# Second product of a gated recurrence and SiLU block: seven half-size products against three one-pass products of exact parts

## The chip, the cores and the metric

The kernel runs on one core of a Trainium2 chip. The time is device microseconds of that core for one execution of the whole program. Names used below: TensorE (PE; PEld is its weight load), VectorE (DVE), ScalarE (ACT), GpSimd (POOL) and SyncE (SP), which only issues transfers.

## The reference

Two blocks follow one another. The first is a complex gated recurrence over 768 steps, for 4 batches of 8 heads with 48 dimensions; the second is a two-layer network with SiLU on the 3072 tokens:

```python
scale = np.minimum(mag, 0.999) / (mag + 1e-06)        # mag = |a_re + i a_im|
for t in range(S):
    new_re = ar * S_re - ai * S_im
    new_im = ar * S_im + ai * S_re
    S_re, S_im = (new_re + kv, new_im)                # kv: outer product of k[t], v[t]
    y[:, :, t] = np.einsum('bhd,bhde->bhe', q[:, :, t], S_re)
x = attn_out.transpose(0, 2, 1, 3).reshape(B * S, H * D)   # 3072 x 384
h = x @ w_in                                          # 384 x 2048: the first product
g = h * (1.0 / (1.0 + np.exp(-h)))
return (g @ w_out).astype(np.float32)                 # 2048 x 384: the second product
```

## The kernel before, in words

The sequence is cut into 24 chunks of 128 tokens (n = 0 to 23), the chunks into 12 pairs of 256 tokens (p = 0 to 11). A chunk's recurrence is worked out in a parallel form: magnitudes and angles of the gates on ACT and VectorE (`G0` to `Ga`), running sums of both by TensorE (`L`, `phase`), sines (`trig`), exponentials (`exp`), rotated and scaled q and k (`K`, `Q`), their transposition to T (`tk` and `tq` on VectorE in 32x32 blocks, then 12 transfers `td` from the SP and POOL queues), scores (`w`), a mask on VectorE (`m`), and the output `y` from scores and the state S carried over from four chunks before. ACT copies `y` to xT (`x`), and six small transfers (`xd`) put its last third in place.

For each pair the network then runs in 8 steps (jp = 0 to 7), each over 256 of the 2048 hidden values. `h:p.jp` (L706) is six float32 matmuls of TensorE, which leave twelve records; `g` (L715) is SiLU on ACT into a tile of 128x512; `r:p.jp` (L745) adds the step's part of the second product into PSUM. There are two kinds of `r`. For the first two pairs it is straight: four float32 matmuls of 384 columns (L756). From the third pair on (`WINO = 2`, L110) it is the method of halves (L777): the 256 tokens by two blocks of 128 hidden values, and those by two halves of 192 columns, are treated as a 2x2 by 2x2 product that takes seven products of half size in place of eight (L803, 14 records). It needs four sums of blocks of `g` on VectorE for each step (`gs`, L736), combinations of the weights made once (`wc`, `wl`), and seven additions for each pair when the last step is done (`of`, L807). Every float32 matmul appears as two records.

Chunks from the eighth on have their running sums made from two exact parts: L425 rounds a tile to float32r, L426 takes the rest, and L437 multiplies both parts with a triangle of ones or halves, which a float32r matmul does in one record.

The order of the work is written out by hand as a list of tokens (L912 on); every engine runs its own instructions in the order of that list, and so does every queue of transfers. Weights arrive as pairs of 32-bit words and are turned into float32 at the start (`F` fetches, `R`, `H` and `J` convert). `sm` and `lk` look at the weights once more near the end; a branch after the list falls back to another routine when inputs are extreme.

PSUM has two buffers for `h` (`p_h`), two for attention (`p_m`) and four for the results (`p_o`, later `late_o`). Most tiles of attention have two buffers each. A helper, L292, records every ACT function, and L286 every load of an ACT table.

Of the kernel before, what the change touches and what calls it, by code (L numbers as in the profile page):

```python
# [70 lines left out]
def kernel(  # L71
# [38 lines left out]
    WINO = 2  # L110
    STRAIGHT = 4
    FULL = 6

# [38 lines left out]
    def load_a(n, g, name):  # L152
        p, i = divmod(n, 2)
        if name not in A[p]:
            A[p][name] = flat(pre.tile([C, 2, H, D], F32, tag=name, name=f"{name}{p}", bufs=2))
        b, c = place(n)
        queue_of(g).dma_start(
            out=cut(A[p][name], i).rearrange("p (h d) -> p h d", d=D),
            in_=(a_re if name == "re" else a_im)[b].rearrange("h (c p) d -> p c h d", p=C)[:, c])
# [18 lines left out]
    w2 = consts.tile([C, NJ, DM], F32)  # L178
# [5 lines left out]
    for s in range(DF // WC):  # L184
# [3 lines left out]
        for j in range(s * WC // C, (s + 1) * WC // C):  # L188
            blocks.append((w2[:, j], (2, j // 2), [(0, w_out[ts(j, C)])]))
# [48 lines left out]
    def small(n):  # L238
# [3 lines left out]
        if n < NT and w.dtype != F32:  # L242
            raw = pre.tile([C, 2, H, D], F32, tag=("re", "im")[n % 2], name=f"small{n}", bufs=2)
# [175 lines left out]
    def in_two(n, x):  # L419
# [3 lines left out]
        t = room("left").tile([C, 2, DM], F32R, tag="part", name=f"{x}_parts{n}", bufs=2)  # L423
# [15 lines left out]
    def carry(n):  # L439
        if place(n)[1] > 0:  # L440
            X[n]["carry"] = att.tile([1, DM], F32, tag="carry", name=f"carry{n}")
# [9 lines left out]
    def turn(n):  # L451
        x = X[n]
        ps = x["phase"]
        x["turn"] = att.tile([C, DM], F32, tag="turn", name=f"turn{n}")
# [91 lines left out]
    def squared(n, i):  # L546
        x = X[n]
        if "sq" not in x:
            x["sq"] = room("left").tile([C, NB, 2 * H, Q], F32, tag="sq", name=f"sq{n}", bufs=2)
# [165 lines left out]
    def silu(p, jp):  # L715
        g = moe.tile([C, 2, T], F32, tag="g", name=f"g{p}_{jp}", bufs=4)
        special(g, A[p]["h", jp], AF.Silu)
        A[p]["g", jp] = g
# [3 lines left out]
    w2v = w2.rearrange("p (j i) (n c) -> p i n j c", i=2, n=2)  # L722

    def combined():

        wc = later["wc"] = room("right").tile([C, 3, NJ // 2, DM // 2], F32, tag="wc", name="wc")
        for out, a, b, op in ((wc[:, 2], w2v[:, 1, 1], w2v[:, 0, 1], ALU.subtract),
                              (wc[:, 1], wc[:, 2], w2v[:, 0, 0], ALU.add),
                              (wc[:, 0], w2v[:, 1, 0], wc[:, 1], ALU.subtract)):
            nc.vector.tensor_tensor(out=out, in0=a, in1=b, op=op)  # L730

    def combined_last():
        nc.vector.tensor_tensor(out=w2v[:, 0, 1], in0=w2v[:, 0, 1], in1=w2v[:, 0, 0],
                                op=ALU.subtract)

    def sums_of(p, jp):  # L736
        g = A[p]["g", jp]
        a11, a12, a21, a22 = (g[:, i, ts(m, C)] for m in range(2) for i in range(2))
        t = room("right").tile([C, 4, C], F32, tag="gs", name=f"gs{p}_{jp}", bufs=2)
        for i, a, b, op in ((0, a21, a22, ALU.add), (1, a11, a21, ALU.subtract),  # L740
                            (2, t[:, 0], a11, ALU.subtract), (3, a12, t[:, 2], ALU.subtract)):
            nc.vector.tensor_tensor(out=t[:, i], in0=a, in1=b, op=op)  # L742
        A[p]["gs", jp] = t

    def result(p, jp):  # L745
        if p >= WINO:
            result_of_halves(p, jp)
            return
        if jp == 0:
            A[p]["o"] = [p_o.tile([C, 2, DM // 2], F32, tag="o",  # L750
                                                                  name=f"o{p}_{m}")
                         for m in range(2)]
        for m in range(2):
            for ji in range(2):
                j = jp * 2 + ji
                nc.tensor.matmul(A[p]["o"][m].rearrange("p n c -> p (n c)"),  # L756
                                 lhsT=A[p]["g", jp][:, ji, ts(m, C)], rhs=w2[:, j],
                                 start=(j == 0), stop=(j == NJ - 1))

    def finish(p):  # L760
        if p >= WINO:
            combine(p)
            return
        for m in range(2):
            ot = moe.tile([C, 2, DM // 2], F32, tag="ot", name=f"ot{p}_{m}")
            nc.scalar.copy(out=ot, in_=A[p]["o"][m])
            store(p, m, {m: ot})

    def store(p, m, ot, half=None):

        b, c = place(2 * p + m)
        to, of = out[ts(b * NCH + c, C)], ot[m].rearrange("p n c -> p (n c)")
        if half is not None:
            to, of = to[:, ts(half, DM // 2)], ot[m][:, half]
        (nc.sync if half is not None else nc.scalar).dma_start(out=to, in_=of)

    def result_of_halves(p, jp):  # L777
        if jp == 0:
            A[p]["o"] = [late_o().tile([C, 2, DM // 2], F32, tag="o", name=f"o{p}_{m}")
                         for m in range(4)]  # L780


        pairs = (0, 5, 4, 3, 1, 6, 2)
        o = [A[p]["o"][i // 2][:, i % 2] for i in map(pairs.index, range(7))]
        final = jp == NJ // 2 - 1
        if p == NP - 1 and jp == NJ // 2 - 2:
            return


        merged = final and p == NP - 1  # L790
        todo = [(i, j) for i in (pairs if merged else range(7))
                for j in ((jp - 1, jp) if merged else (jp,))]
        if merged:

            todo.insert(2, todo.pop(todo.index((1, jp - 1))))
        for i, j in todo:
            g, t = A[p]["g", j], A[p]["gs", j]
            products = ((g[:, 0, 0:C], w2v[:, 0, 0, j]), (g[:, 1, 0:C], w2v[:, 1, 0, j]),
                        (g[:, 1, C:T], later["wc"][:, 0, j]), (t[:, 0], w2v[:, 0, 1, j]),
                        (t[:, 1], later["wc"][:, 2, j]), (t[:, 2], later["wc"][:, 1, j]),  # L800
# [391 lines left out]
```

## Time and profile before

Three runs took 644.46, 644.66 and 646.29 us, median 644.66.

| of the profiled execution | |
|---|---|
| its own time | 644.93 us |
| its span, first to last instruction | 643.2 us |
| mean granted TensorE clock | 0.997 |
| TensorE busy | 628.2 us, 4084 records |
| VectorE busy | 471.1 us, 1009 instructions |
| ACT busy | 360.4 us, 530 instructions, 97.5 of it 76 table loads at L286 |
| GpSimd busy | 212.7 us |
| first product, L711 | 1152 records, 259.5 us |
| second product, straight (L756) and of halves (L803) | 128 and 1120 records |
| sums of `g`, L742 | 320 instructions of 128x128 |
| additions at a pair's end, L816 | 70 instructions of 128x192 |
| transfers | 73.31 MB, 166,224 of 183,447 packets under 512 B |

Busy times of different rows on one engine can overlap, since a matmul is recorded from its start to the end of its way through the array. The mean duration of a record is therefore longer than the time by which it holds up the next one; that time is read from the start of one record to the start of the next. "Idle before" in a row of groups is the time in which the engine stood still ahead of it, with the work that released it.

### The profile page before, as it was taken

The page shows a single profiled execution, that of the slowest core. Times are in us where ns is not written, and L with a number is a line of the kernel's source. Part 1 is how long each engine was busy: PE and PEld are TensorE (multiplying, and loading weights), DVE is VectorE, ACT ScalarE, POOL GpSimd, SP SyncE. Part 2 cuts the span into 40 slices and gives each one's busy share as a digit, 9 for nine tenths or more (in the row PEclk, how much of TensorE's full clock was granted, in tenths as well). Part 3 has the DMA queues.
Part 4 walks back from the last instruction along what each step waited for, and adds up shares of the span by engine and source line. Part 5 has one row for each costly group of instructions (what it writes and reads, how often), then busy time and mean ns, then how long its engine had stood idle before and what let it go on. Part 6 is the DMA issues. An engine that isn't in the chain of part 4 may idle for free.

```text
span 643.2 us, 11607 instructions
## 1 busy us (share of the span) xinstructions
PE 628.2 (98%) x4084; PEld 561.3 (87%) x4084; DVE 471.1 (73%) x1009; ACT 360.4 (56%) x530; POOL 212.7 (33%) x368
## 2 busy tenths in 40 slices
PE   6898999999999999999999999999999999999997
PEld 4777777778999999999999899899999899999996
DVE  5997578885786975896897786776797686585554
ACT  7994777864566666756587258419447542421200
POOL 7442102433553325142063153360352224242000
PEclk9899999999999999999999999999999999999999
DMA  9677474743674476481474554665375438558680
GB/s 168 133 180 160 132 196 133 130 75 73 137 102 81 95 113 99 89 111 26 91 104 68 102 79 64 121 92 89 61 134 79 106 46 162 108 119 175 213 285 29
DMA packets 183447, 73.31 MB, mean 114 GB/s; under 512 B 166224, under 2 KB 171816, under 8 KB 183384
## 3 DMA queue, kind: packets, MB, share of 16 engines
q1 hardware_dynamic: 168424, 50.79, 38.1%
q0 software_dynamic: 11648, 17.20, 17.3%
q10 hardware_dynamic: 3312, 4.52, 1.9%
q8 instruction: 34, 0.56, 0.4%
q14 instruction: 29, 0.24, 0.1%
HBM read 48.90 MB, written 4.79 MB: 83 GB/s over the span
## 4 chain that ended last, share of the span: by engine, by line
PE 84%; ACT 6%; DVE 4%; DMA 3%; issue 1%; SPq 0%; ACTq 0%; POOL 0%; DVEq 0%; POOLq 0%
PE h L711 35%; PE o L803 27%; PE o L756 7%; PE a L569 6%; PE y L596 3%; PE y L599 3%; ACT s L292 1%; ACT L286 1%; DMA v<-in_v_dram 1%; ACT mag L292 1%; PE s L667 1%; DMA xT<-y 1%; PE phase L437 1%; DVE ot L816 1%; PE L L437 1%
## 5 line engine op out<-in xcount | busy, mean ns | idle before, releaser
L711 PE MATMUL h<-xT,w 128*128 128x256 f32 x1152 | 259.5, 379 | 1.0 <-DMA xT<-y 0.6
L711 PEld LDWEIGHTS h<-xT,w 128*128 128x128 f32 x1152 | 217.0, 190 | 31.8 <-ACT g L292 1.2
L292 ACT ACTIVATE g<-h 128x512 f32<-128x512 f32 x96 | 56.2, 595 | 157.8 <-PE h L711 138.7
L557 POOL DMA_DIRECT2D T<-sq x120 | 77.5, 653 | 102.8 <-PE o L803 32.5
L286 ACT ACT_TABLE_LOAD x76 | 97.5, 1283 | 13.5 <-DVE ot L816 8.6
L503 POOL DMA_DIRECT2D dec<-ends x48 | 30.7, 644 | 149.5 <-DMA ends<-eq 141.6
L803 PE MATMUL o<-w,gs 128*128 128x192 f32 x320 | 77.9, 326 | 0.0
L803 PE MATMUL o<-w,g 128*128 128x192 f32 x320 | 66.2, 329 | 0.0
L803 PE MATMUL o<-wc,gs 128*128 128x192 f32 x320 | 64.9, 326 | 0.0
L685 POOL DMA_DIRECT2D S<-ssq x84 | 46.0, 555 | 37.7 <-DVE ssq L674 28.4
L803 PEld LDWEIGHTS o<-w,gs 128*128 128x128 f32 x320 | 56.3, 190 | 0.1
L742 DVE TENSOR_TENSOR gs<-g 128x128 f32<-128x128 f32 x160 | 38.7, 282 | 23.8 <-ACT g L292 18.5
L803 PEld LDWEIGHTS o<-w,g 128*128 128x128 f32 x320 | 53.6, 190 | 2.7 <-issue 0.7
L803 PEld LDWEIGHTS o<-wc,gs 128*128 128x128 f32 x320 | 54.2, 190 | 0.0
L569 PE MATMUL a<-T 96*128 96x128 f32 x384 | 50.3, 278 | 0.8 <-ACT T L561 0.3
L577 DVE TENSOR_TENSOR w<-a,upto_r 128x512 f32<-128x512 f32 x48 | 32.7, 687 | 24.8 <-PE a L569 22.1
L569 PEld LDWEIGHTS a<-T 96*128 96x128 f32 x384 | 47.3, 191 | 3.8 <-issue 1.1
L756 PE MATMUL o<-w,g 128*128 128x384 f32 x128 | 43.6, 488 | 0.0
L608 POOL DMA_DIRECT2D xT<-y x30 | 14.9, 504 | 84.5 <-ACT y L644 84.5
L803 PE MATMUL o<-wc,g 128*128 128x192 f32 x160 | 38.9, 326 | 0.0
L756 PEld LDWEIGHTS o<-w,g 128*128 128x128 f32 x128 | 24.0, 190 | 15.2 <-issue 0.4
L816 DVE TENSOR_TENSOR ot<-o,ot 128x192 f32<-128x192 f32 x70 | 21.5, 351 | 20.5 <-ACT ot L812 14.5
(121 smaller groups left out, 971.2 us busy)
## 6 DMA issues: line engine op xcount, KB each, us to landing
T<-sq SPq DMA_DIRECT2D x120, 64.0 KB
T<-sq POOLq DMA_DIRECT2D x120, 64.0 KB, 4.2
raw<-in_moe_w_out_dram SPq DMA_DIRECT2D x16, 384.0 KB
small<-in_moe_w_in_dram SPq DMA_DIRECT2D x16, 384.0 KB
small<-in_moe_w_out_dram SPq DMA_DIRECT2D x16, 384.0 KB
raw<-in_moe_w_in_dram SPq DMA_DIRECT2D x24, 192.0 KB
out_dram<-ot ACTq DMA_DIRECT2D x23, 192.0 KB
im<-in_a_im_dram SPq DMA_DIRECT2D x16, 192.0 KB
```

The source lines that it names most:

```text
L286: nc.scalar.preload_act_table_set(SETS[of][0])
L292: nc.scalar.activation(out=out, in_=in_, func=func, **kw)
L503: nc.gpsimd.dma_start(out=x["dec"][a * D:(a + 1) * D], in_=ends[n].rearrange("(h d) -> d h", d=D))
L557: (nc.gpsimd if a % 2 else nc.sync).dma_start(out=to[ts(b, Q), :, a], in_=X[n]["sq"][ts(a, Q), b])
L569: nc.tensor.matmul(ps[:, h], lhsT=x["kT"][:, hh * HH + h], rhs=x["qT"][:, hh * HH + h], start=True, stop=True)
L577: nc.vector.tensor_tensor(out=x["w", hh], in0=x["a", hh], in1=upto.unsqueeze(1).to_broadcast([C, HH, C]), op=ALU.mult)
L685: (nc.gpsimd if g % 2 else nc.sync).dma_start(out=to[ts(b, Q), r, :, e], in_=sq[ts(g, Q), :, b, 0:e.stop - e.start])
L711: nc.tensor.matmul(ps[:, ji], lhsT=w1[:, dc, ts(jp * 2 + ji, C)], rhs=A[p]["xT"][:, dc], start=(dc == 0), stop=(dc == ND - 1))
L742: nc.vector.tensor_tensor(out=t[:, i], in0=a, in1=b, op=op)
L756: nc.tensor.matmul(A[p]["o"][m].rearrange("p n c -> p (n c)"), lhsT=A[p]["g", jp][:, ji, ts(m, C)], rhs=w2[:, j], start=(j == 0), stop=(j ...
L803: nc.tensor.matmul(o[i], lhsT=a, rhs=b, start=(jp == 0 and i < 4), stop=(final and j == jp and i in ((5, 3, 6, 2) if p == NP - 1 else (4, ...
L816: nc.vector.tensor_tensor(out=to, in0=a, in1=b, op=ALU.add)
```

## The change

From the fourth pair on (`PARTS = 3`) the second product is taken apart differently; the third pair becomes straight, and the halves with their sums, combinations and additions are gone. Each of `g` and the weights is split into a head (its bits above the lowest twelve) and a rest. With the rest of the weights scaled by 4096 ("fine"), the heads rounded to float32r ("coarse", "head"), and two differences `d` (of `g`) and `t` (of the weights), two accumulators are formed for each chunk: v from d·t, and u from head·coarse plus tail·fine. The result is (1 + 1/4096)·u − v/4096. Every operand is float32r, so that each step has twelve one-pass matmuls of 384 columns.

For each step VectorE makes the head (`ga`), the tail (`gb`) and the difference (`gc`), and ACT copies the head to float32r (`gr`). The three forms have one buffer each (`PBUF = 1`); in the last pair some steps use buffers of attention that are free by then (`HOMES`). The weights' parts are made once (`wh`, `wq`, `wd`, `ws`, `we`); their differences are kept in DRAM (`wk`), and each step loads its difference from there, 384 KB on the SP queue into one of two buffers (`lw`). The end of a pair is a multiplication on ACT (`ov`) and one fused operation on VectorE (`oj`) for each chunk, in two halves for the last pair. `re`, `im`, `part`, `sq`, `turn` and `carry` get one buffer in place of two, and `w2` becomes a ring of nine tiles. The whole list of tokens is in a new order.

```diff
-    WINO = 2
+    PARTS = 3
+    FINER = 2.0 ** -12
...
+    GBUF = 4
+    PBUF = 1
...
-    w2 = consts.tile([C, NJ, DM], F32)
+    w2_pool = Ring(consts, NJ // 2 + 1)
+    w2 = [w2_pool.tile([C, 2, DM], F32, tag="w2", name=f"w2_{jp}") for jp in range(NJ // 2)]
...
-            x["sq"] = room("left").tile([C, NB, 2 * H, Q], F32, tag="sq", name=f"sq{n}", bufs=2)
+            x["sq"] = room("left").tile([C, NB, 2 * H, Q], F32, tag="sq", name=f"sq{n}", bufs=1)
...
+    def head(dst, src):
+        nc.vector.tensor_scalar(out=dst.bitcast(I32), in0=src.bitcast(I32), scalar1=-4096,
+                                scalar2=None, op0=ALU.bitwise_and)
+
+    def difference(dst, tail, whole):
+        nc.vector.scalar_tensor_tensor(out=dst, in0=tail, scalar=-1 / FINER, in1=whole,
+                                       op0=ALU.mult, op1=ALU.add)
+
+    HOMES = (0, 1, 2, 0, 2, 0, 1, 1)
...
+    def w_head(jp):
+        W["head", jp] = temp(f"w_head{jp}", 2 * DM)
+        head(W["head", jp], w2[jp])
+
+    def w_rounded(jp):
+        nc.scalar.copy(out=coarse(jp), in_=W["head", jp])
...
+        nc.vector.tensor_tensor(out=W["rest", jp], in0=w2[jp], in1=W["head", jp], op=ALU.subtract)
...
+        difference(t, W["rest", jp], W["head", jp])
...
+        nc.scalar.mul(t, W["rest", jp], 1 / FINER)
...
+        nc.sync.dma_start(out=second_d[jp].bitcast(I32), in_=W["diff", jp].bitcast(I32))
+
+    def w_loaded(p, jp):
+        t = A[p]["diff", jp] = room("right").tile([C, 2, DM], F32R, tag="diff",
+                                                  name=f"diff{p}_{jp}", bufs=2)
+        nc.sync.dma_start(out=t.bitcast(I32), in_=second_d[jp].bitcast(I32))
+
+    def g_form(p, jp, name):
+        home_of = HOMES[jp] if p == NP - 1 else 0
+        if home_of == 0:
+            t = room("right").tile([C, 2, T], F32R, tag=name, name=f"{name}{p}_{jp}", bufs=PBUF)
...
+    def g_head(p, jp):
+        A[p]["temp", jp] = temp(f"g_head{p}_{jp}", 2 * T)
+        head(A[p]["temp", jp], A[p]["g", jp])
+
+    def g_rounded(p, jp):
+        nc.scalar.copy(out=g_form(p, jp, "head"), in_=A[p]["temp", jp])
+
+    def g_tail(p, jp):
+        t = g_form(p, jp, "tail")
+        nc.vector.tensor_tensor(out=t, in0=A[p]["g", jp], in1=A[p]["temp", jp], op=ALU.subtract)
+
+    def g_diff(p, jp):
+        difference(g_form(p, jp, "gd"), A[p]["tail", jp].bitcast(F32), A[p]["temp", jp])
...
+    def result_of_parts(p, jp):
+        x = A[p]
+        a, b, d, t = (x[name, jp] for name in ("head", "tail", "gd", "diff"))
+        last_ = jp == NJ // 2 - 1
+        for m in range(2):
+            u, v_ = (x["o"][2 * m + i].rearrange("p n c -> p (n c)") for i in range(2))
+            for ji in range(2):
+                nc.tensor.matmul(v_, lhsT=d[:, ji, ts(m, C)], rhs=t[:, ji],
+                                 start=(jp == 0 and ji == 0), stop=(last_ and ji == 1))
+            for ji in range(2):
+                j = jp * 2 + ji
+                nc.tensor.matmul(u, lhsT=a[:, ji, ts(m, C)], rhs=W["coarse"][:, j],
+                                 start=(jp == 0 and ji == 0), stop=False)
+                nc.tensor.matmul(u, lhsT=b[:, ji, ts(m, C)], rhs=W["fine", jp][:, ji],
+                                 start=False, stop=(last_ and ji == 1))
...
+    def o_scaled(p, m):
+        ot = A[p]["ot", m] = moe.tile([C, 2, DM // 2], F32, tag="ot", name=f"ot{p}_{m}")
+        nc.scalar.mul(ot, A[p]["o"][2 * m + 1], -FINER)
+
+    def o_joined(p, m):
...
+            nc.vector.scalar_tensor_tensor(out=ot[:, n], in0=u[:, n], scalar=1 + FINER,
+                                           in1=ot[:, n], op0=ALU.mult, op1=ALU.add)
...
+                gr:7.3 turn:19 lw:7.3 w:17.1 m:17.1 v:17 y:17 x:17 gb:7.3 gc:7.3 g:7.7 G7:10 G4:10
+                s:17 ss:17 r:7.3 td:18 w:18.1 w:18.0 lw:7.4 gb:7.4 gr:7.4 gc:7.4 r:7.4 k:19 xd:8
...
+                lw:11.4 lk:30 lk:31 ck2:0 ck3:0 ck4:0 h:11.4 gr:11.6 r:11.6 g:11.4 h:11.7 ga:11.5
+                ga:11.4 gr:11.4 gb:11.4 gc:11.4 r:11.4 g:11.7 ga:11.7 gb:11.5 gc:11.5 lw:11.5
+                gb:11.7 gc:11.7 gr:11.5 r:11.5 gr:11.7 lw:11.7 r:11.7 ov:11.0 ov:11.1 oj:11.0
+                oj:11.1
```

## The prediction

> **What bounds the kernel now.** I read the page first: the busy shares and the chain that ended last.
>
> ```profile
> PE 628.2 (98%) x4084; PEld 561.3 (87%) x4084; DVE 471.1 (73%) x1009; ACT 360.4 (56%) x530; POOL 212.7 (33%) x368
> PE   6898999999999999999999999999999999999997
> PE 84%; ACT 6%; DVE 4%; DMA 3%; issue 1%; SPq 0%; ACTq 0%; POOL 0%; DVEq 0%; POOLq 0%
> PE h L711 35%; PE o L803 27%; PE o L756 7%; PE a L569 6%; PE y L596 3%; PE y L599 3%; ACT s L292 1%; ACT L286 1%; DMA v<-in_v_dram 1%; ACT mag L292 1%; PE s L667 1%; DMA xT<-y 1%; PE phase L437 1%; DVE ot L816 1%; PE L L437 1%
> ```
>
> TensorE holds 84% of the chain, the second product (L803, L756) 34%. Busy time can't tell TensorE's rate, so I take the rate from where it runs without a gap, in the chain in order of time:
>
> ```profile
> 101.03 2.58 PE o L756 x8
> ...
> 164.62 4.55 PE o L803 x28
> 169.17 2.59 PE h L711 x12
> ```
>
> One `r` of halves is 14 records: 4.55/2 = 2.275 us, 162.5 ns each. A straight `r` is 2.58 us (322.5 ns a record); an `h` 2.59 us (216 ns). From 60.76 us on, at the first `r`, the chain is nearly all TensorE. The busy times by stage say how near the others are:
>
> ```profile
> core 0: us, PE busy (x) PEld busy (x) DVE busy (x) ACT busy (x) POOL busy (x), PEclk, DMA share, GB/s
> 300.00:350.00 50.00, 50.00 (x331) 47.16 (x331) 42.84 (x96) 33.81 (x48) 18.40 (x33) 1.00 0.55 88
> 400.00:450.00 50.00, 49.51 (x347) 46.25 (x345) 34.50 (x77) 25.16 (x39) 15.22 (x27) 1.00 0.60 97
> ```
>
> TensorE is full, VectorE has 7 to 15 us of 50 free. Shortening a product shortens the end, as long as VectorE keeps ahead.
>
> **What the Trainium skill says.** "TensorE: Matmul & The Clock Gate", "Back-to-back issue gap", gives a warm matmul N/2.4 + 2.5 ns: 162.5 ns for 384 columns. Two-pass records agree (322.5 is twice 161). "VectorE: DVE Perf Modes", the perf-mode tier table, has float32 `tensor_scalar` at twice the rate of `tensor_tensor`; the trace agrees (432 against 692 ns at 512 elements, below). "DMA: Bandwidth & Descriptors", "Issuing engines are not separate DMA queues": all queues share 16 engines, so the new loads meet the rearranging of T and S.
>
> **The change, part by part.** *TensorE.* The one-pass form exists before: the exact parts of L437, two records of 384 columns. Two timeline answers around 206 us:
>
> ```profile
> 205.45 0.38 PE L711 MATMUL h<-xT,w 128*128 128x256 f32 x1
> 205.48 0.70 PE L437 MATMUL phase<-th_parts,upto_r 128*128 128x384 f32 x2
> ```
> ```profile
> 205.85 0.33 PE L437 MATMUL phase<-th_parts,upto_r 128*128 128x384 f32 x1
> 206.02 0.59 PE L711 MATMUL h<-xT,w 128*128 128x256 f32 x2
> ```
>
> From 205.45 to 206.02 is 0.57; less the 0.216 of the `h` it is 0.354 for two, 177 ns each (the second alone 170). No row shows more than two in sequence. If the surplus over 162.5 belongs to the change of form, twelve in sequence take 1.95 us; if to each matmul, 2.12. I take 170 ns, 2.04 us. Gain: 72 × (2.275 − 2.04) = 16.9 us. The third pair goes back to the straight product: 8 × (2.58 − 2.275) = 2.4 us lost. Net −14.5 (ends −21.0 and −8.7). `h`, `w`, `y`, `s`, L and phase keep their numbers, and ACT's table loads stay the same within one (counted along both orders).
>
> *VectorE and ACT.* Rows used, by line and shape:
>
> ```profile
> L742 DVE TENSOR_TENSOR gs<-g 128x128 f32<-128x128 f32 x160 | 38.7, 282 | 23.8 <-ACT g L292 18.5 <-PE o L803 5.1
> L577 DVE TENSOR_TENSOR w<-a,upto_r 128x512 f32<-128x512 f32 x48 | 32.7, 687 | 24.8 <-PE a L569 22.1 <-PE y L596 2.5
> L816 DVE TENSOR_TENSOR ot<-o,ot 128x192 f32<-128x192 f32 x70 | 21.5, 351 | 20.5 <-ACT ot L812 14.5 <-DMA xT<-y 3.9 <-PE o L803 0.6
> L49 DVE SCALAR_TENSOR_TENSOR w<-raw,w 128x512 int32<-128x512 int32 x12 | 8.3, 692 | 0.4
> L401 DVE TENSOR_SCALAR re<-re 128x768 f32<-128x768 f32 x11 | 6.2, 566 | 0.0
> L47 DVE TENSOR_SCALAR w<-raw 128x512 int32<-128x512 int32 x12 | 5.2, 432 | 1.9 <-DMA raw<-in_moe_w_in_dram 1.9
> L561 ACT COPY T<-tp 96x512 f32<-96x512 f32 x16 | 8.5, 583 | 0.9 <-PE tp L541 0.9
> ```
>
> Per product VectorE gets `ga` 0.43, `gb` 0.69 and `gc` 0.69, 1.81 us, for four sums of 0.28 to 0.29, 1.14: +0.67, ×72 = 48.2. Per pair two `oj` of 0.56 replace seven additions of 0.351: −1.34, ×9 = −12.1. The third pair loses its sums and additions: −11.6. The weights cost 8 × (0.566 + 0.955 + 0.955) = 19.8 (L401; 128x768 like L333), less `wc` and `wl`, 7.0. Sum +37: VectorE 471 to 508. ACT gets 72 × 0.58 + 16 × 0.84 + 20 × 0.48 − 10 × 0.32 = +62: 360 to 422. Both are hidden behind TensorE so long as they keep up. Summing start-to-start costs (0.36, 0.70, 0.61 for the three parts; other tokens likewise) along the new order from r:3.0 to r:9.0, VectorE has 278 us of work and TensorE 299: 93%, where before it was 76%.
>
> *The new wait.* With PBUF = 1 `gb`, `gc` and `gr` of a product start after the product before has been read. Queued behind a waiting `gb` on VectorE are the masks (`w`), T's transposes and `ut`/`ul` of later chunks, for which `y` and phase wait. After the release `gb` and `gc` take 1.3 us plus a semaphore; the order puts at least an `h` (2.6), `w:18` pair (1.8) or `y` (1.85) there, except between products of the last pair, which have other homes. Over the 63 intervals up to r:10.7 I took VectorE's work from one `gb` to the next against TensorE's from one product to the next: at the row costs none waits, eleven are left with under 0.7 us spare, the least 0.34. With VectorE's costs 7% up the waits sum to 2.6 us, with 10% to 8 us. Since this count leaves out VectorE's own waits, I put 3 us (ends 0 and 10).
>
> *Loads.* 72 loads of 384 KB (28 MB) and 8 stores. The nearest, `small`, are issued at 617.99 and reduced at 621.23, 3.2 us; in dense sequence they come about 1 us apart. 72 × 1 us raises the DMA share from about 0.55 to 0.67. Two buffers give a load the time from product k−2's end to product k: 9.4 us on average, at least 6.5 up to the eleventh pair, so it is hidden; without cover a product would wait up to 3 us. On SP it stands between T's transfers, whose waits for `tq` it inherits. In the last pair the load for r:11.7 waits for r:11.4, with only r:11.5 (2.0) between: 3.4 − 2.0 = 1.4 us shown. Put 1.5 (0 to 3).
>
> *Buffers cut to one, order of the start.* `sq`, `turn`, `part`, `carry`, `re`, `im` now wait for their last reader. Up to x:3 ACT, which bounds the start, has 41.1 us against 39.1, but TensorE has one more `r` behind it by then (2.6 us): even, ±3. The tail (ACT's multiplication, two half `oj`, store) is as long as the old one's last additions.
>
> Sum against the profiled execution, 644.93 (span 643.2 and 1.7 around it; the runs' median is 644.66): −14.5 + 3 + 1.5 = −10, so 635.
>
> **Rivals.** *VectorE becomes the bound* (the slower side): from the fourth to the ninth pair it already has 93%; waits for L, phase and scores in an in-order queue that may not run ahead of `gb` could use 15%: 278 becomes 320 against 299, 21 us, so 644.9 − 14.5 + 1.5 + 21 = 653. It decides once TensorE's waits there pass 13 us, about 0.3 us a product. For: single forms and the thin spare above. Against: no interval is short at the row costs, and in the old order stages of 85% VectorE left TensorE full. *One pass at 162.5 and no new wait*: 644.9 − 21.0 + 1.5 = 625. For: the page's rate; against: 170 to 177 at L437. *The diff loads come late*: behind T's transfers on SP, 0.25 us per product, 18 us: 650. Against: T's landing (4.2 us from POOL) fits with the rest into 9.4. *It isn't one pass*: at 322 ns a matmul r is 3.86, 114 us more: 759. Against: L437 leaves one record per matmul, L434's float32 two.
>
> **How the numbers follow.** Forecast 0.58 (its own range 629 to 641); full one-pass rate 0.13; VectorE 0.20; late loads 0.07; not one pass 0.02. 624 to 650 leaves out most of the last and the upper half of VectorE's case, with a little of the others: 2 in 10. No change is taken as within 0.3%, 2 us. Faster: 0.55 + 0.13 + 0.04 from mild forms of the two wait cases = 0.72; same 0.06; slower 0.22.
>
> **What would show it.** Right: twelve records per product in about 2.04 us, TensorE's digits at 9 from slice 5 on, VectorE about 508 us busy, `gb` waiting for TensorE rather than TensorE for `gc`. Wrong: idle TensorE before the second product released by VectorE (`gd`), ACT (`head`) or the `diff` DMA; a product of 2.12 us or more; a first `r` later than 63 us.

## The result, and the profile after

| | before | after |
|---|---|---|
| runs beside each other | 13 | 13 |
| median | 645.13 us | 636.97 us |
| lowest to highest | 644.12 to 646.99 us | 633.51 to 643.15 us |
| ratio of the times, 95% interval | | 0.9878 (0.9852 to 0.9905) |
| the profiled execution, span | 644.93 us, 643.2 us | 642.44 us, 640.7 us |

The changed kernel is 8 us faster. One of its 13 runs, 643.15, is more than 1.5% above its fastest and is left out of the ratio. Its runs lie 9.6 us apart where those of before lie 2.9 apart, and the profiled one is among its longest, 5.5 us above the median: it probably shows more stalls than a median run has.

The page after, with the busy shares, TensorE's slices and the transfers:

```profile
PE 620.5 (97%) x3892; PEld 542.2 (85%) x3892; DVE 513.7 (80%) x875; ACT 417.1 (65%) x629; POOL 214.7 (34%) x368
...
PE   6899999999999999999999989999999998999996
...
DMA packets 195111, 104.75 MB, mean 163 GB/s; under 512 B 167520, under 2 KB 173240, under 8 KB 195048
...
q1 hardware_dynamic: 179944, 82.25, 55.7%
```

TensorE's busy time has fallen by 7.7 us, to 620.5; VectorE's has risen to 513.7, ACT's to 417.1. Two of TensorE's slices in the middle are no longer 9. SP's queue q1 now takes 55.7% of the time of the 16 transfer engines (38.1% before). Over the spans that is 356.9 − 245.1 = 111.8 us more, for 72 loads and 8 stores of 384 KB: **1.40 us of all 16 engines for each**. This takes the queue's other transfers to last as long as before. They do in a kernel further down that has neither loads nor stores (three products directly): 38.8% of 632.4 us, 245.4.

The groups of the second product, in the form name, count | busy, mean ns | idle before:

```profile
L835 PE MATMUL o<-coarse,head 128*128 128x384 f32 x280 | 94.7, 338 | 0.0
L837 PE MATMUL o<-fine,tail 128*128 128x384 f32 x280 | 94.4, 337 | 0.0
L831 PE MATMUL o<-diff,gd 128*128 128x384 f32 x280 | 82.0, 374 | 2.5 <-DMA diff<-w_diffs 2.2
L798 ACT CAST head<-g_head 128x512 fp32r<-128x512 f32 x70 | 43.0, 615 | 61.3 <-PE o L835 40.6
L802 DVE TENSOR_TENSOR tail<-g,g_head 128x512 fp32r<-128x512 f32 x70 | 47.9, 684 | 29.8 <-PE o L837 29.4
L731 DVE SCALAR_TENSOR_TENSOR gd<-tail,g_head 128x512 fp32r<-128x512 f32 x70 | 48.2, 689 | 1.9
```

Each matmul leaves one record. The forms wait for TensorE (40.6 us ahead of `head`, 29.4 ahead of `tail`), not TensorE for the forms: what stands ahead of L831 is a transfer. The rate shows in the starts of the records. From the timeline of one product (start us, duration us):

```profile
525.64 0.34 PE L835 MATMUL o<-coarse,head 128*128 128x384 f32 x1
525.82 0.33 PE L837 MATMUL o<-fine,tail 128*128 128x384 f32 x1
525.99 0.34 PE L835 MATMUL o<-coarse,head 128*128 128x384 f32 x1
526.16 0.34 PE L837 MATMUL o<-fine,tail 128*128 128x384 f32 x1
```

Three steps in 0.52 us. Over the products the median step is 175 ns. The 21 products that lie between two `h` hold TensorE for 2.093 us in the median (2.087 to 2.226), from the start of the last `h` record before them to that of the next, less that record's own 0.216; before it was 2.275.

The busy times by stage, with the columns as before:

```profile
300.00:350.00 50.00, 49.91 (x339) 46.24 (x338) 46.72 (x80) 37.00 (x55) 17.59 (x31) 1.00 0.88 180
350.00:400.00 50.00, 48.22 (x325) 44.09 (x324) 44.08 (x75) 36.86 (x53) 24.12 (x43) 1.00 0.75 145
400.00:450.00 50.00, 48.96 (x340) 45.61 (x340) 44.50 (x77) 36.74 (x54) 18.11 (x31) 1.00 0.82 166
```

VectorE, third, has 3 to 6 us of 50 left, and TensorE is full from 300 to 350 all the same. It stands still where VectorE is no busier: 1.8 us from 350 to 400. The last column but one has changed most: the transfer engines are busy 0.75 to 0.88 of the time, 0.55 and 0.60 before. What TensorE waits for from 160 us on, in the view of waits (us in total, times, longest), after:

```profile
PE o L831 <- DMA diff<-w_diffs: 2.2, 1, 2.2
PE a L574 <- DMA re<-in_a_re_dram: 1.8, 1, 1.8
PE y L601 <- DVE L L492: 1.1, 1, 1.1
PE a L574 <- DVE turn L462: 1.0, 1, 1.0
...
PE o L831 <- DVE gd L731: 0.4, 1, 0.4
```

And before:

```profile
PE h L711 <- DMA xT<-y: 0.6, 2, 0.4
PE h L711 <- ACT g L292: 0.4, 1, 0.4
PE a L569 <- DVE ssq L674: 0.3, 1, 0.3
```

So 7 us of waits stand where there were 1.3. L574 reads T, so "re" and "turn" beside it only name what came last by the profile. The longest wait, at 528 us, is for a load itself.

### The profile page after: what moved, and what is told of

Same layout as the page of the kernel before. It is cut to its first block, busy times and chain, and to the rows that moved or that the text cites. A ratio compares the mean times of both kernels' runs of the same rounds, so it can differ in the third digit from the quotient of the medians.

```text
span 640.7 us, 11617 instructions
## 1 busy us (share of the span) xinstructions
PE 620.5 (97%) x3892; PEld 542.2 (85%) x3892; DVE 513.7 (80%) x875; ACT 417.1 (65%) x629; POOL 214.7 (34%) x368
## 3 DMA queue, kind: packets, MB, share of 16 engines
q1 hardware_dynamic: 179944, 82.25, 55.7%
## 4 chain that ended last, share of the span: by engine, by line
## 5 line engine op out<-in xcount | busy, mean ns | idle before, releaser
L835 PE MATMUL o<-coarse,head 128*128 128x384 f32 x280 | 94.7, 338 | 0.0
L837 PE MATMUL o<-fine,tail 128*128 128x384 f32 x280 | 94.4, 337 | 0.0
L831 PE MATMUL o<-diff,gd 128*128 128x384 f32 x280 | 82.0, 374 | 2.5 <-DMA diff<-w_diffs 2.2
L798 ACT CAST head<-g_head 128x512 fp32r<-128x512 f32 x70 | 43.0, 615 | 61.3 <-PE o L835 40.6
L802 DVE TENSOR_TENSOR tail<-g,g_head 128x512 fp32r<-128x512 f32 x70 | 47.9, 684 | 29.8 <-PE o L837 29.4
L831 PEld LDWEIGHTS o<-diff,gd 128*128 128x128 f32 x280 | 50.5, 188 | 7.5 <-DVE kr L529 2.4
L820 PEld LDWEIGHTS o<-w,g 128*128 128x128 f32 x192 | 36.2, 190 | 22.4 <-DVE w L49 0.2
L574 PEld LDWEIGHTS a<-T 96*128 96x128 f32 x384 | 47.1, 191 | 6.7 <-issue 2.9
L837 PEld LDWEIGHTS o<-fine,tail 128*128 128x128 f32 x280 | 52.8, 189 | 0.0
L835 PEld LDWEIGHTS o<-coarse,head 128*128 128x128 f32 x280 | 52.7, 188 | 0.0
L574 PE MATMUL a<-T 96*128 96x128 f32 x384 | 48.9, 276 | 3.7 <-DMA re<-in_a_re_dram 1.8
L731 DVE SCALAR_TENSOR_TENSOR gd<-tail,g_head 128x512 fp32r<-128x512 f32 x70 | 48.2, 689 | 1.9
```

Of the source, the lines that this page charges most:

```text
L574: nc.tensor.matmul(ps[:, h], lhsT=x["kT"][:, hh * HH + h], rhs=x["qT"][:, hh * HH + h], start=True, stop=True)
L731: nc.vector.scalar_tensor_tensor(out=dst, in0=tail, scalar=-1 / FINER, in1=whole, op0=ALU.mult, op1=ALU.add)
L802: nc.vector.tensor_tensor(out=t, in0=A[p]["g", jp], in1=A[p]["temp", jp], op=ALU.subtract)
L831: nc.tensor.matmul(v_, lhsT=d[:, ji, ts(m, C)], rhs=t[:, ji], start=(jp == 0 and ji == 0), stop=(last_ and ji == 1))
L835: nc.tensor.matmul(u, lhsT=a[:, ji, ts(m, C)], rhs=W["coarse"][:, j], start=(jp == 0 and ji == 0), stop=False)
L837: nc.tensor.matmul(u, lhsT=b[:, ji, ts(m, C)], rhs=W["fine", jp][:, ji], start=False, stop=(last_ and ji == 1))
```

## The experiments

Three theories. **A**: TensorE's time sets the end; the change gains what the shorter product saves, less what the 72 loads of 384 KB cost. **B**: VectorE, with its forms in single buffers, holds TensorE up. **C**: the new order and the single buffers of attention cost or bring time of their own. A has two forms: the loads cost because SP stands still for them (A1), or because their bytes take the shared transfer engines (A2). Kernels of one table part ran beside the same runs of before, whose median is given.

| | median (lowest to highest), us | ratio to before (95%) |
|---|---|---|
| *before: 644.60* | | |
| the changed kernel again | 637.79 (635.24 to 643.23) | 0.9887 (0.9854 to 0.9919) |
| no loads | 633.31 (632.66 to 633.77) | 0.9814 (0.9799 to 0.9830) |
| no `gd` | 637.29 (634.94 to 642.06) | 0.9898 (0.9864 to 0.9932) |
| new order, all straight | 667.60 (665.71 to 668.02) | 1.0350 (1.0334 to 1.0366) |
| *before: 644.93* | | |
| loads on ACT's queue | 644.89 (640.43 to 651.07) | 0.9988 (0.9973 to 1.0003) |
| three products directly | 634.14 (632.53 to 634.48) | 0.9826 (0.9810 to 0.9842) |
| the same, two of each form | 633.75 (632.57 to 634.52) | 0.9829 (0.9814 to 0.9843) |
| *before: 645.67* | | |
| waits without bytes | 632.95 (631.98 to 635.11) | 0.9793 (0.9773 to 0.9813) |
| bytes without waits | 636.65 (634.78 to 641.20) | 0.9868 (0.9834 to 0.9902) |
| loads on ACT's queue, mended | 641.01 (638.28 to 642.32) | 0.9918 (0.9895 to 0.9941) |
| *before: 646.00* | | |
| bytes from POOL's queue | 641.26 (639.54 to 642.45) | 0.9929 (0.9908 to 0.9951) |

### The changed kernel again, and without its loads

> The changed kernel again, as the yardstick of the runs beside it. Theory A (TensorE sets the time; twelve one-pass matmuls take 2.09 us; the loads of the differences make other transfers late and cost some us more), theory B (VectorE's new work behind single forms sets the waits) and theory C (the new order and the single buffers of attention cost, whatever the products are) all expect about 637 us, 0.988 of before.

```diff
     def w_loaded(p, jp):
+        if p > PARTS or jp > 3:
+            A[p]["diff", jp] = A[PARTS]["diff", 2 + jp % 2]
+            return
```

> 68 of the 72 loads of differences are left out: every product from the fifth of the fourth pair on takes one of two differences that stay, so v is not that of its own weights. TensorE, VectorE and ACT do the same work. A: the waits on transfers go, TensorE's work alone is left: 645 less 10.7 of shorter products plus about 1 of other waits, 634 to 635, ratio 0.982 to 0.984, with DMA share back near 0.57 in the middle. B and C: as the changed kernel, 637.

Without the loads the time falls by 4.5 us (637.79 − 633.31), and its runs lie 1.1 us apart in place of 8. The stage in which the changed kernel stood still is full again; from the busy times by stage of the kernel without loads:

```profile
350.00:400.00 50.00, 49.98 (x336) 46.06 (x335) 46.09 (x79) 38.93 (x55) 25.52 (x44) 1.00 0.67 111
```

VectorE is busier here than in the changed kernel (46.09 against 44.08). It is not VectorE that stops TensorE. What does can be followed around 370 us. The timeline of the changed kernel run again, SP, POOL and TensorE:

```profile
370.54 0.25 SPq L505 DMA_DIRECT2D ends<-eq  x1
...
371.50 4.00 SPq L562 DMA_DIRECT2D T<-sq  x6
...
372.22 1.27 POOL L508 DMA_DIRECT2D dec<-ends  x2 [11.14 <-DMA ends<-eq]
373.71 3.85 POOL L562 DMA_DIRECT2D T<-sq  x6 [0.21 <-issue]
...
383.77 1.54 PE L574 MATMUL a<-T 96*128 96x128 f32 x7 [2.32 <-DMA S<-ssq]
```

And without the loads:

```profile
365.18 0.24 SPq L505 DMA_DIRECT2D ends<-eq  x1
...
367.80 1.39 POOL L508 DMA_DIRECT2D dec<-ends  x2 [8.41 <-DMA ends<-eq]
368.92 4.76 SPq L562 DMA_DIRECT2D T<-sq  x6
369.43 4.14 POOL L562 DMA_DIRECT2D T<-sq  x6 [0.24 <-DVE w L582]
...
380.76 1.95 PE L574 MATMUL a<-T 96*128 96x128 f32 x16
```

A transfer of one row, `ends`, leaves SP 5.4 us later with the loads, though what it reads is ready at about the same time (ACT's `eq` ends at 365.70 and 365.15). POOL's queue, in order, waits for it to land and only then sends its half of T, and the scores come 2.3 us late. SP's own waits from 362 to 372 us say what held `ends`:

```profile
SPq L505 <- DMA out_dram<-ot: 5.0, 1, 5.0
```

`out_dram` is a store of ACT's queue that `ends` has nothing to do with. In this trace all transfers of SP and ACT count on the same eight semaphores (101 to 103, 114 to 118), and each waits before it is issued until the transfer that used its semaphore before has landed. From 200 to 600 us SP waits for such and other transfers 1.4 us before, 30.0 with the change and 13.7 without its loads. This wait alone doesn't stop TensorE. The kernel of three direct products, further down, moves no loads, and there `ends` stands behind the same store too:

```profile
SPq L505 <- DMA out_dram<-ot: 4.2, 1, 4.2
```

It leaves at 367.66, POOL's half of T at 370.68 (373.71 above), POOL's transfers of T land 3.5 us after their issue in the median of that stage (5.0 above), and TensorE doesn't stop. With the loads T leaves 3.0 us later and takes 1.5 us longer. Whether the waits (A1) or the bytes (A2) make the cost is what the later experiments ask.

### VectorE relieved

```diff
     def g_diff(p, jp):
-        difference(g_form(p, jp, "gd"), A[p]["tail", jp].bitcast(F32), A[p]["temp", jp])
+        A[p]["gd", jp] = A[p]["tail", jp]
```

> The third form is left out: the tail stands in for the difference d, so v is not the real one; 72 operations of 0.69 us, 50 us, are taken from VectorE, and a product waits for one VectorE operation after the release in place of two. TensorE and transfers are as in the changed kernel. B: the waits for VectorE go, 632 or less. A and C: within 1.5 us of the changed kernel.

```profile
PE 617.4 (97%) x3892; PEld 541.4 (85%) x3892; DVE 467.8 (74%) x803; ACT 416.8 (66%) x629; POOL 216.8 (34%) x368
```

VectorE has 46 us less to do (467.8 against 514.0) and the time is the same, 637.29 against 637.79. B falls as far as VectorE's amount of work goes; the single buffers follow below.

### The new order and single buffers alone

```diff
-    PARTS = 3
+    PARTS = 12
...
-            "ga": g_head, "gr": g_rounded, "gb": g_tail, "gc": g_diff,
-            "lw": w_loaded, "ov": o_scaled, "oj": o_joined,
+            "ga": lambda p, jp: None, "gr": lambda p, jp: None, "gb": lambda p, jp: None,
+            "gc": lambda p, jp: None, "lw": lambda p, jp: None, "ov": o_scaled,
+            "oj": lambda p, m: None,
```

(The tokens of the weights' parts do nothing either, `o_scaled` copies and stores, and `g` keeps eight buffers.)

> The new order and the single buffers of attention alone: all pairs straight (eight records of 322.5 ns, 2.58 us), none of the parts made, no differences stored or loaded, g in eight buffers. Against before ten pairs lose 80 x (2.58 - 2.275) = 24.4 us on TensorE. A and B: 645 + 24.4 = 669.5, less whatever waits of before go: 668 to 670, ratio about 1.037. C: 672 or more.

```profile
PE 648.9 (98%) x3604; PEld 499.1 (75%) x3604; DVE 372.4 (56%) x615; ACT 366.3 (55%) x541; POOL 213.4 (32%) x368
```

Before, 80 products were of halves. Made straight they cost 80 × (2.58 − 2.275) = 24.4 us, so the old order would take 644.6 + 24.4 = 669.0. Measured: 667.6. New order and single buffers of attention together are worth about −1.4 us, give or take 1; they cost nothing, and C falls. VectorE is lighter here (372.4 us busy, 513.7 in the changed kernel), so their cost beside a busy VectorE isn't read from this run. The kernel without loads leaves little room for it: −10.7 us of shorter products (worked out below) and −1.4 make 632.5 of 644.6, and 633.31 was measured.

### The price of a one-pass matmul

> The changed kernel with 128 matmuls put behind its end, in eight groups of 16, each with its own weights unless said otherwise: float32r of 128, 256, 384 and 512 columns; 384 columns with 64 columns of weights; 384 with the same weights throughout; float32 of 384; bfloat16 of 384. If the 175 ns are a fixed surplus of each float32r matmul, the first four step by 53.3 ns: 68, 122, 175, 229. If they are a lower rate, they are 0.456 ns a column: 58, 117, 175, 233. If the loading of weights sets them, 128 and 256 columns also take about 175, and narrow weights take less. If accumulation or the change of PSUM bank in the product sets them, 384 columns take 162.5 here. float32 is expected at two records of 322, bfloat16 at 162.

```diff
+    def price(_):
+        w = W["coarse"].rearrange("p j x -> p (j x)")
+        ps = p_h.tile([C, 2, T], F32, tag="h", name="price").rearrange("p i x -> p (i x)")
+        half_ = w.bitcast(mybir.dt.bfloat16)
+        for k, (of, n, cols, step) in enumerate((
+                (w, 128, C, C), (w, 256, C, C), (w, 384, C, C), (w, 512, C, C), (w, 384, 64, C),
+                (w, 384, C, 0), (w.bitcast(F32), 384, C, C), (half_, 384, C, C))):
+            for i in range(16):
+                nc.tensor.matmul(ps[0:cols, 0:n], lhsT=of[:, i * step:i * step + cols],
+                                 rhs=of[:, 0:n], start=True, stop=True)
...
```

Sixteen matmuls of each kind, alone at the end of the program (661.17 us in all); the mean step from start to start:

| operands | columns | ns a record |
|---|---|---|
| float32r | 128 | 112 |
| float32r | 256 | 119 |
| float32r | 384 | 173.5 |
| float32r | 512 | 229 |
| float32r, 64 columns of weights | 384 | 173 |
| float32r, the same weights each time | 384 | 173 |
| float32, two records each | 384 | 322.5 |
| bfloat16 | 384 | 162.5 |

The sum, 16 × (0.112 + 0.119 + 0.1735 + 0.229 + 0.173 + 0.173 + 2 × 0.3225 + 0.1625) = 28.6 us, is what the timeline gives for all of them (28.77). The surplus of about 11 ns over 162.5 belongs to every float32r matmul of 384 columns. It doesn't shrink with the weights (a load of 64 columns of them is recorded with 133 ns, one of 128 with 188, and the matmul takes 173 either way), it doesn't come from an accumulation or a change of bank (every one of these starts a new sum in one bank), and bfloat16 doesn't have it. What causes it isn't shown. Hence 173 to 175 in the products.

### Three products directly, without loads and differences

Head times coarse, head times rest and tail times coarse go into one accumulator, tail times rest is left out; `gd`, the differences, their loads and the fused end of a pair are gone.

```diff
-            u, v_ = (x["o"][2 * m + i].rearrange("p n c -> p (n c)") for i in range(2))
+            u = x["o"][2 * m].rearrange("p n c -> p (n c)")
...
+                nc.tensor.matmul(u, lhsT=a[:, ji, ts(m, C)], rhs=W["coarse"][:, j],
+                                 start=(jp == 0 and ji == 0), stop=False)
+                nc.tensor.matmul(u, lhsT=a[:, ji, ts(m, C)], rhs=W["fine", jp][:, ji],
+                                 start=False, stop=False)
+                nc.tensor.matmul(u, lhsT=b[:, ji, ts(m, C)], rhs=W["coarse"][:, j],
+                                 start=False, stop=(last_ and ji == 1))
...
-        nc.scalar.mul(t, W["rest", jp], 1 / FINER)
+        nc.scalar.copy(out=t, in_=W["rest", jp])
```

> The product of tail and rest is left out (about 2^-24 of the whole), and head x coarse, head x rest and tail x coarse go into one accumulator, with the rest of the weights not scaled: still twelve one-pass matmuls, but no third form, no differences to make, store or load, and a plain copy at a pair's end. Theory A: as without the loads, 632 to 634, ratio 0.980 to 0.983, and less spread than the changed kernel. If the loads were not the cause but only moved the timing, 637.

It takes 634.14 us, ratio 0.9826, and so **beats both kernels**: 10.8 us under before, and 2.7 to 3.9 under the kernels that move the bytes from SP (0.9826 against 0.9868, the unread loads below, and 0.9887, the changed kernel). TensorE has the same twelve records for a product. It is full where the changed kernel stood still, and the transfer engines are busy 0.65 of that stage:

```profile
350.00:400.00 50.00, 49.93 (x335) 46.02 (x333) 41.08 (x71) 38.98 (x56) 25.51 (x45) 1.00 0.65 111
```

With two buffers of each form:

```diff
-    PBUF = 1
+    PBUF = 2
```

> The same with two buffers for head and tail. Theory A (TensorE sets the time, the single forms are covered by other work): within 1 us of the version with one. Theory B: 2 us or more below it.

633.75 against 634.14: no difference. The single forms of head and tail, for which the prediction had put 3 us, cost nothing here that these runs can tell. This kernel has no `gd`; in the changed kernel itself the profile shows 0.4 us of TensorE's waits for it.

### Bytes or waits

Two kernels take A apart. The first keeps every load and its waits, but 68 of the 72 load 16 KB in place of 384, into differences that stay:

```diff
+        if p > PARTS or jp > 3:
+            W["turn"] = W.get("turn", 1) + 1
+            t = A[p]["diff", jp] = A[PARTS]["diff", 2 + W["turn"] % 2]
+            nc.sync.dma_start(out=t[:, :, 0:16].bitcast(I32),
+                              in_=second_d[jp][:, :, 0:16].bitcast(I32))
+            return
```

> The waits of the loads without their bytes: as in the run without loads two differences stay (v is not that of its own weights), but each of the 68 loads is still issued at its place on SP, waits for the product that last read its buffer and is waited for, with 16 KB in place of 384. Theory A1 (the harm is that SP stands still in front of the loads, with T's and S's transfers behind them): 636 to 638, ratio about 0.988. Theory A2 (the harm is the bytes): 633 to 634.5, 0.982.

The second is the kernel of three direct products, which needs no loads, with all 72 put back into tiles that nothing reads (the differences are made and stored again too, eight operations on VectorE and eight stores):

```diff
+    def unread(p, jp):
+        t = room("right").tile([C, 2, DM], F32R, tag="diff", name=f"unread{p}_{jp}", bufs=2)
+        nc.sync.dma_start(out=t.bitcast(I32), in_=second_d[jp].bitcast(I32))
...
-            "lw": w_loaded, "ov": o_scaled, "oj": o_joined, "at": lambda p, i: gates_atan(p, i),
+            "lw": unread, "ov": o_scaled, "oj": lambda p, m: None, "at": lambda p, i: gates_atan(p, i),
```

> The bytes without the waits: the version with three direct products, with the differences made and stored and all 72 loads of 384 KB at their places on SP, into two tiles that no product reads, so that a load waits only for an earlier load. The product of tail and rest is left out as before. A1: 633.5 to 635, ratio 0.982 to 0.984. A2: 636 to 638.

The same stage with small loads, from the busy times by stage:

```profile
350.00:400.00 50.00, 49.98 (x335) 45.95 (x334) 46.04 (x78) 38.83 (x56) 24.82 (x44) 1.00 0.63 101
```

With the bytes that nobody reads, from the same view and from TensorE's waits:

```profile
350.00:400.00 50.00, 46.98 (x319) 43.10 (x318) 38.09 (x65) 35.83 (x52) 24.64 (x43) 1.00 0.89 144
```
```profile
PE a L574 <- DMA re<-in_a_re_dram: 3.0, 1, 3.0
```

The number of loads and their waits cost nothing (ratio 0.9793, no slower than without loads, 0.9814). The bytes cost (0.9868 − 0.9826) × 645 = 2.7 us where no TensorE work waits for them (give or take 2.4, from the two intervals), with a 3 us stop ahead of T's scores once more. So A2 holds, in that the cost needs the bytes. With the 28 MB the transfers of S from POOL's queue take 3.2 to 3.4 us in the median from issue to landing, in the kernels without them 2.1 to 2.5.

One thing is left between the two: the bytes also make SP wait longer for transfers that have not landed, 38 us from 200 to 600 us here, 12 with small loads. The same 28 MB sent by POOL, on other semaphores, were to take that away:

```diff
-        nc.sync.dma_start(out=t.bitcast(I32), in_=second_d[jp].bitcast(I32))
+        nc.gpsimd.dma_start(out=t.bitcast(I32), in_=second_d[jp].bitcast(I32))
```

> As e9_bytes_no_waits (the same 72 loads of 384 KB into tiles that nothing reads, no TensorE wait; tail times rest left out of the sum), but the loads are issued from POOL's queue, so that SP's transfers follow one another as without the loads. In the traces SP stands still for transfers that have not landed 12 to 18 us between 200 and 600 us without the bytes, 38 us in e9_bytes_no_waits, often behind a store of the ACT queue: each transfer of SP and ACT takes one of eight counters in turn and waits until the transfer that had it before has landed. Bytes themselves (the engines are shared, whoever issues): as e9_bytes_no_waits, about 636.5 us, ratio 0.987, single waits of 1 to 3 us of TensorE for T remain. The counters of SP and ACT (the loads turn them faster): as three_direct, about 634 us, ratio 0.983, SP's waits for transfers back at 18 us or less. POOL's own time (72 issues in front of its half of T) could add to either; then POOL is busy beyond 216 us and TensorE waits behind it.

SP's waits for stores of ACT's queue are gone; its other waits for transfers, most of them behind fetches of weights, still come to 25 us (18 in the kernel of three direct products). The stage from 350 to 400 us is full. Its busy times, and POOL's waits from 200 to 600 us:

```profile
350.00:400.00 50.00, 49.93 (x335) 45.98 (x334) 40.98 (x70) 39.02 (x56) 30.73 (x53) 1.00 0.82 163
```
```profile
POOL unread L777 <- DMA unread<-w_diffs: 28.3, 12, 7.0
```

Yet the time, 641.26 us, is longer, not shorter. POOL is busy 256.5 us (215.9 with the loads on SP), and now it stands 28 us behind loads that have not landed, with T and S queued behind. Freeing SP only moved the queueing. That the stop at 381 us is gone doesn't show that it hung on SP's semaphores: TensorE comes to that point later here (the `h` ahead of the scores starts at 380.06, 378.70 in the changed kernel), so T has more time. How much of the 2.7 to 4.5 us is the semaphores' and how much the slower landing stays open: POOL's standing still covers both in this run.

### The loads from ACT's queue

Two tries to take the loads off SP, each load behind the copy that already waits for the same product:

```diff
-    def w_loaded(p, jp):
+    def w_loaded(p, jp, queue=None):
+        if queue is None and p < NP - 1 and (p, jp) >= (PARTS, 3):
+            return
...
     def g_rounded(p, jp):
         nc.scalar.copy(out=g_form(p, jp, "head"), in_=A[p]["temp", jp])
+        q_, j_ = (p, jp + 1) if jp < NJ // 2 - 1 else (p + 1, 0)
+        if q_ < NP - 1 and (q_, j_) >= (PARTS, 3):
+            w_loaded(q_, j_, nc.scalar)
```

> The loads of differences of all but the first three and the last eight products are issued from ACT's queue, right behind the copy of the head for the product before, which waits for the same product as the load does; the SP queue no longer stands still for them. Theory A1 (the loads harm because SP waits in front of them, 65 us in the profile, and T's and S's transfers stand behind): most of the 4.5 us come back, 633.5 to 635. Theory A2 (they harm because 28 MB more share the 16 engines): no better than the changed kernel, 636 to 639.

644.89 us, as before the change. One cause was of the experiment's making: moving the fourth load exchanged two buffers, and ACT waited 2.9 us at 236 us for a product. With `(PARTS, 4)` in place of `(PARTS, 3)`:

> The loads on ACT's queue once more, from the sixth product of parts on: the run before had moved one load ahead of its predecessor, so that two loads used one buffer in turn and ACT stood still for 2.9 us. If that one wait and the gap of TensorE behind it (2.5 us) were the whole difference to a cure, 634 to 637; if the loads do as much harm behind ACT as behind SP, because ACT's queue is as full of work that others wait for, 638 to 644.

641.01 us. By the ratios that is 2 us more than from SP (0.9918 against 0.9887), but the two intervals overlap; better it is not. The trace shows one full chain, from a wait of SP between 330 and 341 us:

```profile
SPq L161 <- DMA diff<-w_diffs: 3.3, 1, 3.3
```

through the timeline of ACT, VectorE and TensorE:

```profile
343.55 0.84 ACT L297 ACTIVATE s<-im 128x768 f32<-128x768 f32 x1 [2.85 <-DMA im<-in_a_im_dram]
...
344.43 0.96 DVE L322 SCALAR_TENSOR_TENSOR s<-s,s 128x768 f32<-128x768 f32 x1 [3.39 <-ACT s L297]
...
346.17 0.69 DVE L807 TENSOR_TENSOR tail<-g,g_head 128x512 fp32r<-128x512 f32 x1
...
347.64 0.62 PE L836 MATMUL o<-diff,gd 128*128 128x384 f32 x2 [2.83 <-DVE gd L731]
```

SP waits 3.3 us for a load of ACT's queue that has its semaphore before it sends a gate's `re` and `im`; ACT stands 2.85 us for `im`; VectorE stands behind ACT with the tail queued after `s`; and TensorE 2.83 us behind the tail's difference. It is named "gd", and begins at a load.

## Why the prediction was right

It said 635.0 us, 624 to 650, faster; measured 636.97. The path was right: TensorE sets the time, its product is shorter in one pass, and VectorE keeps ahead. That the number came within 2 us is in part luck, since errors of 3 to 4 us cancelled. By its steps:

- **TensorE's gain: right in kind, mis-sized.** The step that failed is the value of 170 ns between 162.5 and 177, taken from the second of two records. Measured 175 in sequence (a mean of 174.4 over a product), and 173.5 by itself: 2.093 us a product in place of 2.04. The gain is 72 × (2.275 − 2.093) = 13.1 in place of 16.9, less 2.4 for the third pair: −10.7, inside the stated ends (−21.0, −8.7). Twelve records of this length show the single pass.
- **VectorE and ACT: right.** 508 and 422 us were forecast, 513.7 and 417.1 measured. VectorE stays hidden; with 46 us less of it nothing is gained. The trace's 432 against 692 ns, set beside a factor of two for `tensor_scalar` over `tensor_tensor`, is a factor of 1.6, and both rows are of int32 data, the second a `scalar_tensor_tensor`. The new operations keep that factor (426 ns for the head, 684 for the tail), so the sum came out right all the same.
- **The new wait: too dear.** 3 us put; TensorE waits 0.4 us for `gd`, and a second buffer of head and tail brings nothing in the kernel of three direct products. The order leaves room enough, as the count at the row costs had said.
- **The loads: wrong step.** "Hidden", with 1 us of the engines each, forgot what the load does to other transfers. Measured 1.40 us each; the share rose to 0.75 to 0.88 rather than 0.67, and the loads cost 2.7 us (bytes alone) to 4.5 us (all). Of the 7 us of waits in the profile 2.2 are at a load itself, which the prediction had named as a sign of being wrong; otherwise T, S and a gate's input come late. The rival "the diff loads come late" had the right resource, transfers, and a wrong place and size (18 us, in front of the product). For the last load, put at 1.5 us, neither profile of the changed kernel shows a wait of TensorE. That all queues share the 16 engines, as the prediction quoted from the Trainium skill ("DMA: Bandwidth & Descriptors", "Issuing engines are not separate DMA queues"), agrees with the runs: from ACT's or POOL's queue the same bytes cost no less than from SP's, and from POOL's 4 us more (0.9929 against 0.9868).
- **Buffers and order: right as even.** −1.4 us, give or take 1, by the straight kernel.

The measured sum: −10.7 (TensorE) − 1.4 (order) + 4.5 (loads) = −7.6, where the runs show −8.2 and, the second time, −6.8. The forecast's −10 was 2 us too good, by 3.8 too much from TensorE and 2.5 to 3 too little for the loads, partly paid back by the 3 us for waits that did not come and by the order.

The Trainium skill's "TensorE: Matmul & The Clock Gate" (section "Back-to-back issue gap") gives N/2.4 + 2.5 ns. It fits bfloat16 here exactly (162.5 at 384), and half of a float32 record within two nanoseconds (161), but not float32r, which takes 11 ns more. There the measurement decides.

## What to carry to other kernels

When a kernel bound by one engine is given more traffic, price the traffic against the small transfers that other stages hang on, not only against the time until the load itself is needed: here 28 MB cost 2.7 to 4.5 of some 12 us gained, and leaving them out by another split of the product was worth more than either queue they were moved to. Take the price of a matmul from a long sequence of its own form. And follow a late transfer back to the queue that issued it: the engine or tile that a wait names may be three queues away from its start.

## What was not expected of the hardware

- A float32r matmul has its own price: 0.43 ns a column plus 9 ns from 256 columns on, and hardly less at 128 columns (112) than at 256 (119).
- The loads make the time scatter. Kernels with the 28 MB on SP have runs 6 to 10 us apart, those without them, or with small loads, 1 to 3.
- A stop of TensorE can cost more than its length. In all fourteen traces the granted clock changes only between 1.00 and 0.50, and within a trace its changes lie whole multiples of 3.41 us apart. Cut into periods of 3.41 us at these edges, the profile of the changed kernel has, around its stop of 2.2 us at 528 (the clock is the last value but two):

```profile
528.76:532.17 3.41, 1.52 (x9) 1.56 (x10) 0.87 (x2) 0.39 (x2) 1.49 (x3) 1.00 0.23 80
532.17:535.59 3.42, 3.42 (x11) 2.97 (x10) 1.96 (x4) 1.10 (x2) 0.00 (x0) 0.50 0.45 129
```

  The longer stop of 3.0 us in the kernel with unread bytes falls across an edge, and the clock stays:

```profile
378.79:382.20 3.41, 1.93 (x9) 1.35 (x8) 1.80 (x3) 1.44 (x2) 1.82 (x4) 1.00 1.25 154
382.20:385.62 3.42, 1.94 (x16) 1.86 (x16) 0.69 (x1) 2.00 (x4) 0.90 (x2) 1.00 1.26 162
385.62:389.03 3.41, 3.41 (x41) 3.22 (x41) 3.23 (x7) 1.33 (x4) 0.40 (x1) 1.00 0.16 23
```

  The periods in which TensorE was least busy between 60 and 620 us, in all traces:

| kernel | stop of TensorE, us | busy share of its period | clock in the next |
|---|---|---|---|
| the changed kernel again | 2.3 at 381 | 0.32 | 0.50, two periods long |
| loads on ACT's queue | 2.3 at 239 | 0.34 | 0.50 |
| the same, mended | 2.8 at 345 | 0.40 | 0.50 |
| the changed kernel | 2.2 at 528 | 0.45 | 0.50 |
| loads on ACT's queue | 2.8 at 352 | 0.46 | 1.00 |
| bytes from POOL's queue | 1.7 at 601 | 0.51 | 1.00 |
| bytes without waits | 3.0 at 381 | 0.57 and 0.57 | 1.00 |

  In these traces, then, it is the busy share of a fixed period that goes with the fall, not the length of the stop, with the border near 0.45 (in the first 40 us and the last 20, periods of 0.43 to 0.47 went either way). The edges lie elsewhere in every trace, so that the same stop costs nothing more in one run and, by an estimate from half the clock over one or two periods, 1.7 or 3.4 us more in another. This is part of the scatter: of the changed kernel's two sets of runs, the five above 641 us have mean clocks of 0.988 to 0.995, those below 638 us 0.993 to 0.998. It isn't the whole cost of the loads: three of the second set have 0.997, as runs without loads do, and still take 635.2 to 638.7 us, where the runs without loads take 632.7 to 633.8. Why the clock once stayed low for a second, full period isn't shown. The Trainium skill's "TensorE: Matmul & The Clock Gate", in "Part 1: The HAM clock gate", has the clock fall after an idle window of about 3.4 us that runs freely; length and free running agree with these traces, but the window needn't be idle: with TensorE busy for 0.45 of it the clock fell.
